# A small product ahead of each run of 448-column products, in an attention and mixing kernel on one core

## The chip, the cores and the metric

The kernel runs on one core of a Trainium2 chip (trn2). The metric is the device time of one execution in microseconds, lower is better; the time of a kernel is the median of several runs. One run of each kernel is also recorded by the hardware profiler, and everything that is said of single instructions below comes from such a record.

## The reference

Two stages in float32. Causal attention over 4 batches of 12 heads, 448 positions of width 64; then a mixing stage on the result x of 448 by 768 for each batch:

```python
scores = where(mask, -1e9, scale * q @ k.T); attn = softmax(scores); x = attn @ v
theta = x @ w_theta                       # 448x768 times 768x768
zr, zi = x * cos(theta), x * sin(theta)
y = w_tok_r @ zr + w_tok_i @ zi           # over the 448 positions
u = x + y
out = u + maximum(u @ w_ch, 0)            # 448x768 times 768x768
```

## The kernel before

All data lie with a channel or a position on the 128 partitions. Float32 accuracy is kept by splitting each operand into a high and a low part of a type that TensorE takes in one pass, and adding three products: high by high, high by low, low by high. So each block of a matrix product is three TensorE instructions with the same output, the first two with the same stationary operand (weights, `lhsT`). Each TensorE instruction of the program (a matmul) becomes two in the record: a load of its 128 weight columns (LDWEIGHTS, on the row of the engine that the profile calls PEld) and the product itself (MATMUL, on PE), also where the weights are those of the instruction before.

The parts that TensorE runs:

- attention: scores (lines 614 and 627, tiles `s`, `t`, `m`), transposes of the softmax weights by a product with the identity (line 672, 128 columns), the sums' transposes (line 646), and the products with v (line 698, 64 weight columns);
- `theta` (line 750): 384 columns a product, six blocks of 128 channels;
- `prep(g)` (lines 809 and 810): four transposes of x for channel block g, 128 columns each;
- `mix(g)` (line 829), for six channel blocks g of each of four batches: seven blocks of positions, three products each, all of 448 columns into one PSUM bank `y` of 512 columns, of which 448 are used and read;
- `pair` (line 927), twice, for two batches each: the last matrix product, done by a scheme that needs seven instead of eight half-size products, each named `product(w, ub, banks, ...)`: nine blocks of three products of 448 columns, into three PSUM banks `cp`, again 448 of 512 columns used. The very last product ends with 18 halves of 224 columns (line 937).

Vector, Scalar and GpSimd engines make the operands of these products and read the banks.

The order of all instructions is set by a planner in the kernel: `P.op` lists an operation with its estimated duration, its buffers and a due time, and `P.order()` simulates the engines and writes the program in the resulting order. A mix's seven operations are seven entries, so operations of the attention or of `theta` are put between them in the first batches; near the end little is left to put between, and the 448-column products follow each other without a break. What an entry emits (the inner function `mm`) is not seen by the planner, only its estimate `3 * pe(S)`.

```python
            for c in range(NTK):
                def mm(c=c):
                    for n, (l, w2) in enumerate(((zh, 0), (zh, 1), (zl, 0))):
                        nc.tensor.matmul(out=y.t[:, 0:S], lhsT=l.t[:, c], rhs=wtk[:, c, w2], ...)
                tick(3 * pe(S))
                P.op("PE", 3 * pe(S), mm, [(zh, i), (zl, i), (bwtk, (c, 0)), (bwtk, (c, 1))], [y])
```

Of the kernel before, what the change touches and what calls it, by code (L numbers as in the profile page):

```python
# [382 lines left out]
def attention_moe_kernel(  # L383
# [9 lines left out]
    nc = tc.nc  # L393
    B, NP, S = kq.shape[0], kq.shape[1], out.shape[2]
# [34 lines left out]
    def buf(ring, shape, dtype=F32, name=None):  # L429
        def make():  # L430
            if ring in ("s", "t", "xo", "m"):
                pool = psum
            elif ring in in_moe:
                pool = moe
            elif ring == "xT":
                pool = xpool
            elif ring == "rd":
                pool = dram
            elif ring in ("ub", "q1", "ot", "wf"):
                pool = o_pool[0]  # L440
            else:
                pool = apool
            return pool.tile(shape, dtype, tag=ring, name=name or ring, bufs=rings[ring])
        return P.buf(ring, make)
# [11 lines left out]
    wtk = wpool.tile([128, NTK, 2, S], F32R, name="wtk")  # L456
# [5 lines left out]
    def pe(n):  # L462
        return {128: 85, 256: 118, 384: 173.7, 448: 203.3, 512: 236}[n]

    def dv(n):
        return n / 0.96 + 68
# [13 lines left out]
    def dma(fns, nbytes, r=(), w=(), pr=None, after=(), row=1792, near=False, act=False):  # L480
        def run():
            for f in fns():
                (nc.scalar if act else nc.sync).dma_start(out=f[0], in_=f[1])
        n = nbytes[0]
        o = P.op("ACT" if act else "SP", 530 if n == 1 else 615.0 * n, run, r, w, lat=0, pr=pr, after=after)
        o.wire = nbytes[1] * (0.047 + 12 / row) / 16 * (1.2 if near else 1.0)
        return o
# [219 lines left out]
    th_last = []  # L707


    def batch(b, t0, rate):  # L710
        x = xT[b]
        R = [buf("R", [128, 4, HW]) for _ in range(2)]
# [4 lines left out]
        def tick(c):  # L717
            clock[0] += c * (KN["MR3"] if b < B - 1 and clock[0] > tau(NH) else rate)
            P.now = clock[0]
# [103 lines left out]
        def mix(g):  # L823
            zh, zl = zs[g]
            y = buf("m", [128, 512], F32, "y")
            for c in range(NTK):
                def mm(c=c):
                    for n, (l, w2) in enumerate(((zh, 0), (zh, 1), (zl, 0))):
                        nc.tensor.matmul(out=y.t[:, 0:S], lhsT=l.t[:, c], rhs=wtk[:, c, w2],  # L829
                                         start=(c == 0 and n == 0), stop=(c == NTK - 1 and n == 2))  # L830
                i = 0 if c < 4 else 1
                tick(3 * pe(S))
                P.op("PE", 3 * pe(S), mm, [(zh, i), (zl, i), (bwtk, (c, 0)), (bwtk, (c, 1))], [y])
            xk = [(x, (g, 0)), (x, (g, 1))]
            P.op("DVE", dv(S), lambda: nc.vector.tensor_tensor(
                out=x.t[:, g], in0=y.t[:, 0:S], in1=x.t[:, g], op=ALU.add), [y], xk)
            if b < B - KN["XT"]:
                dma(lambda: [(spill[b].t[:, g], x.t[:, g])], (1, 229376), xk, [(spill[b], g)])
# [32 lines left out]
    def pair(ba, bb, xa, xb, t0, rate, wb, ws, after, banks, rq, ro, end=False):  # L871
# [44 lines left out]
        def product(w, ub, banks, first, inner=True, half=None):  # L916
            wt, wk = w
            for x in range(NC):
                for y in range(NC):
                    m, c = (y, x) if inner else (x, y)  # L920

                    if m == NC - 1 and not inner:
                        break

                    def mm(m=m, c=c):
                        for n, (w2, a) in enumerate(((0, 0), (0, 1), (1, 0))):
                            nc.tensor.matmul(out=banks[m].t[:, 0:S], lhsT=wt()[:, c, w2, 128 * m:128 * m + 128],  # L927
                                             rhs=ub[c].t[:, a], start=(first and c == 0 and n == 0),
                                             stop=(c == NC - 1 and n == 2), skip_group_check=True)
                    clock[0] += 3 * pe(S) * rate  # L930
                    P.now = clock[0]
                    P.op("PE", 3 * pe(S), mm, [(ub[c], 0), (ub[c], 1)] + wk(c), [banks[m]])
            for z in range(0 if inner else 2):
                for c in range(NC):
                    def mm(c=c, z=z):
                        for n, (w2, a) in enumerate(((0, 0), (0, 1), (1, 0))):
                            nc.tensor.matmul(out=(half if z else banks[NC - 1]).t[:, 0:H2], lhsT=wt()[:, c, w2, 128 * NC - 128:128 * NC],
                                             rhs=ub[c].t[:, a, H2 * z:H2 * z + H2], start=(z == 1 and c == 0 and n == 0),
                                             stop=(c == NC - 1 and n == 2), skip_group_check=True)
                    clock[0] += 330 * rate  # L940
                    P.now = clock[0]
                    P.op("PE", 330, mm, [(ub[c], 0), (ub[c], 1)] + wk(c), [half if z else (banks[NC - 1], 0)])
# [58 lines left out]
        if end:  # L1001
            half = buf("s", [128, 512], F32, "cp")
            P.op("DVE", dv(H2), lambda: nc.vector.tensor_tensor(
                out=u2.t[:, NC - 1, H2:S], in0=Z[NC - 1].t[:, H2:S], in1=u2.t[:, NC - 1, H2:S], op=ALU.add),
# [34 lines left out]
    for b in range(B):  # L1039
        for p in range(NP):  # L1040
            load_pair(NP * b + p)
            attend(NP * b + p)
        if b == B - 1:
            att_ops = [o for o in P.ops[n_att:] if any(u.ring in ATT or u.ring[0] in "ep" for u in o.bufs)]
            P.now = tau(NH)

            def switch():
                att.close()
                o_pool.append(ctx.enter_context(tc.tile_pool(name="o", bufs=1)))
                for n in range(4):  # L1050
                    o_pool.append(o_pool[0].tile([128, NC, 2, HW], F32R, name=f"wa{n}", tag=f"wa{n}"))
            sw = P.op("X", 0, switch, after=att_ops)
            bw = [fixed(None) for _ in range(4)]
            for n in range(4):
                fetch(n, n % 2, 0, n // 2, lambda n=n: o_pool[1 + n], bw[n], TA + KN["E0"] + KN["ER"] * n, [sw])
            ws_t = wth.rearrange("p a b n -> p (a b n)")
            step = NC * 2 * HW
            wv = [ws_t[:, step * i:step * i + step].rearrange("p (c w n) -> p c w n", c=NC, w=2) for i in range(4)]
            bs = [fixed(t) for t in wv]
            wb = [((lambda n=n: o_pool[1 + n]), (lambda c, n=n: [(bw[n], (c, 0)), (bw[n], (c, 1))])) for n in range(4)]  # L1060
            ws = [((lambda i=i: wv[i]), (lambda c, i=i: [(bs[i], (c, 0)), (bs[i], (c, 1))])) for i in range(4)]
            first = pair(1, 2, xT[1], xT[2], TA + KN["O0"], KN["OR"], wb, ws, [sw],
                         (("s", "s", "t"), ("t", "xo", "s"), ("s", "t", "t"), ("xo", "s", "s")), "q1", "ot")
            next(first)
        t0 = tau(KN["HL"] + H * b + 2) + KN["M0"]
        end = batch(b, t0, KN["MR"] if b < B - 1 else KN["MR2"])
        if b < NC:
            channel(b, end + KN["C0"])
# [79 lines left out]
```

## Time and profile before

| | |
|---|---|
| time, median of 3 runs | 455.54 us (455.35 to 457.2) |
| time of the profiled execution | 456.17 us |
| its span, first to last instruction | 454.4 us |
| outside of the span | 1.8 us |
| TensorE products (PE) | 444.1 us busy, 2651 instructions |
| TensorE weight loads (PEld) | 367.0 us busy, 2651 instructions |
| VectorE, ScalarE, GpSimd | 362.5, 254.4, 50.5 us busy |
| granted TensorE clock, mean | 0.996 |

Busy time is the union of an engine's instructions. A product's recorded duration holds its way through the array as well, so that consecutive products overlap in the record: the time that one costs is the step from its start to the next one's start, and a merged row of n products gives it as its length over n. The chain of waits counts that step.

### The profile page before, as it was taken

What the parts mean: (1) busy time and instruction counts of PE and PEld (TensorE: products, weight loads), DVE (VectorE), ACT (ScalarE), POOL (GpSimd) and SP (SyncE); (2) the same over time, 40 slices, a digit from 0 to 9 for tenths busy, and PEclk for the clock granted to TensorE, in tenths of its full rate; (3) what the DMA queues carried; (4) which work ended last, traced back from release to release, by engine and by line L of the source; (5) the groups of instructions that cost most, each with busy time, mean ns of one, the idle gap of its engine ahead of it and who ended that gap; (6) DMA issues with size and microseconds to landing.
All of it is one profiled execution on the core that took longest, in us unless ns stands there. A gap on an engine that the chain in (4) does not pass through costs nothing.

```text
span 454.4 us, 7734 instructions
## 1 busy us (share of the span) xinstructions
PE 444.1 (98%) x2651; PEld 367.0 (81%) x2651; DVE 362.5 (80%) x953; ACT 254.4 (56%) x634; POOL 50.5 (11%) x51
## 2 busy tenths in 40 slices
PE   7979999999999999999999999999999999999996
PEld 3646667887777897887877998799999999999996
DVE  3999999669899856598979447896676999879976
ACT  5988797579965545289657217872125725322320
POOL 1022322000000010000002000021000023332320
PEclk9998999999999999999999999999999999999999
DMA  8886665213355363032350400132422331126114
GB/s 285 321 275 223 189 217 159 95 48 109 111 184 200 111 228 100 6 101 93 100 183 27 160 0 12 42 115 79 179 70 71 87 120 53 38 93 212 61 40 143
DMA packets 32391, 56.10 MB, mean 123 GB/s; under 512 B 11576, under 2 KB 23136, under 8 KB 32352
## 3 DMA queue, kind: packets, MB, share of 16 engines
q1 hardware_dynamic: 32064, 55.35, 37.5%
q8 instruction: 21, 0.34, 0.3%
q10 hardware_dynamic: 288, 0.26, 0.2%
q14 instruction: 18, 0.15, 0.1%
HBM read 42.34 MB, written 11.69 MB: 119 GB/s over the span
## 4 chain that ended last, share of the span: by engine, by line
PE 91%; DMA 4%; DVE 3%; issue 1%; SPq 0%; ACT 0%; DVEq 0%; ACTq 0%
PE y L829 23%; PE th L750 20%; PE cp L927 17%; PE xo L698 9%; PE t L672 8%; PE s L627 4%; PE s L614 3%; PE t L627 2%; PE xp L809 2%; DMA raw<-w_theta 2%; DMA kk<-kq 1%; DMA raw<-w_tok 1%; DVE e L633 1%; PE xo L646 1%; PE m L627 1%; PE xp L810 1%
## 5 line engine op out<-in xcount | busy, mean ns | idle before, releaser
L750 PE MATMUL th<-wth,xs 128*128 128x384 f32 x528 | 105.9, 345 | 0.0
L829 PE MATMUL y<-wtk,zh 128*128 128x448 f32 x336 | 101.0, 381 | 0.0
L750 PEld LDWEIGHTS th<-wth,xs 128*128 128x128 f32 x528 | 90.3, 188 | 5.0 <-issue 1.8
L636 ACT ACTIVATE e<-e,sm 128x384 f32<-128x384 f32 (+2 forms) x144 | 72.0, 501 | 28.0 <-DVE sm L633 27.4
L829 PEld LDWEIGHTS y<-wtk,zh 128*128 128x128 f32 x336 | 59.5, 188 | 6.4 <-issue 1.8
L829 PE MATMUL y<-wtk,zl 128*128 128x448 f32 x168 | 61.5, 366 | 0.0
L698 PE MATMUL xo<-pt,vs 128*64 128x448 f32 (+3 forms) x384 | 47.7, 387 | 0.3 <-ACT rs L648 0.3
L672 PE MATMUL t<-ident,e 128*128 128x128 f32 x288 | 44.7, 277 | 0.8 <-ACT pt L500 0.8
L698 PEld LDWEIGHTS xo<-pt,vs 128*64 128x64 f32 x384 | 25.1, 136 | 24.4 <-issue 14.3
L500 ACT COPY pt<-t 128x384 f32<-128x384 f32 (+2 forms) x73 | 34.5, 489 | 18.2 <-PE t L672 16.0
L927 PE MATMUL cp<-ub,wth 128*128 128x448 f32 x207 | 44.1, 367 | 0.0
L633 DVE CUSTOM_DVE_ANT_0 e<-s,mask 128x128 f32<-128x128 f32 (+2 forms) x94 | 37.0, 415 | 8.7 <-PE s L627 7.7
L672 PEld LDWEIGHTS t<-ident,e 128*128 128x128 f32 x288 | 34.4, 141 | 10.6 <-issue 2.9
L927 PEld LDWEIGHTS cp<-ub,wth 128*128 128x128 f32 x207 | 38.8, 188 | 3.7 <-issue 0.2
L927 PE MATMUL cp<-ub,wa 128*128 128x448 f32 x162 | 35.5, 367 | 0.0
L829 PEld LDWEIGHTS y<-wtk,zl 128*128 128x128 f32 x168 | 31.5, 188 | 2.8
L927 PEld LDWEIGHTS cp<-ub,wa 128*128 128x128 f32 x162 | 30.2, 188 | 2.6
L502 DVE COPY pt<-t 128x512 f32<-128x512 f32 (+2 forms) x47 | 27.5, 593 | 2.6 <-PE t L672 1.7
L636 ACT ACTIVATION_READ_ACCUMULATOR e<-e,sm 128x1 f32 x144 | 27.0, 188 | 0.0
L627 PE MATMUL s<-kk 64*128 64x384 f32 (+2 forms) x188 | 26.7, 399 | 0.0
L508 POOL TENSOR_TENSOR zc<-zc 128x384 f32<-128x384 f32 x6 | 6.0, 1009 | 178.6 <-DVE zc L530 178.0
L627 PEld LDWEIGHTS s<-kk 64*128 64x128 f32 x188 | 17.9, 190 | 9.1 <-issue 1.6
(115 smaller groups left out, 683.9 us busy)
## 6 DMA issues: line engine op xcount, KB each, us to landing
kk<-kq SPq DMA_DIRECT2D x23, 480.0 KB, 6.8
vs<-v SPq DMA_DIRECT2D x24, 256.0 KB, 3.7
raw<-w_theta SPq DMA_DIRECT2D x6, 768.0 KB
raw<-w_ch SPq DMA_DIRECT2D x6, 768.0 KB
wd<-zc SPq DMA_DIRECT2D x6, 768.0 KB
wf<-wd SPq DMA_DIRECT2D x24, 192.0 KB, 2.6
raw<-w_tok SPq DMA_DIRECT2D x7, 448.0 KB
rb<-rd SPq DMA_DIRECT2D x24, 112.0 KB, 2.8
```

The lines of the kernel that those rows point to most:

```text
L500: alts.append((e, ac(n, 0 if psum else 1), lambda: nc.scalar.copy(out=o(), in_=i())))
L502: alts.append((e, dv(n) if psum else dv2(n), lambda: nc.vector.tensor_copy(out=o(), in_=i())))
L614: nc.tensor.matmul(out=s.t[:, 0:S], lhsT=kp.t[:, S + MQ:S + KW], rhs=kp.t[:, 0:S])
L627: nc.tensor.matmul(out=s.t[:, c0:c0 + w], lhsT=kp.t[own, S + 128 * i:S + 128 * i + 128], rhs=kp.t[own, 0:w])
L633: P.op("DVE", dv(w) + 8, lambda m0=m0, c0=c0, w=w, s=s, e=e, c=c: nc.vector.tensor_tensor_reduce(out=e.t, in0=s.t[:, c0:c0 + w], in1=mask[ ...
L636: P.op("ACT", ac(w, 2.5), lambda e=e, c=c: nc.scalar.activation(out=e.t, in_=e.t, func=AF.Exp, scale=-1.0, bias=sm.t[:, 0, c:c + 1], accum ...
L672: nc.tensor.transpose(ps.t[:, 128 * n:128 * n + 128], e.t[:, c:c + 128], ident)
L698: nc.tensor.matmul(out=xo.t[64 * a:64 * a + 64, 128 * j:S], lhsT=vs.t[:, c:c + D], rhs=pt.t[:, a, slot(j):slot(j) + w], start=(j == 0), st ...
L750: nc.tensor.matmul(out=th.t[:, 0:HW], lhsT=l, rhs=wth[:, p, w2, c0:c0 + HW], start=(p == 0 and n == 0), stop=(p == KD - 1 and n == len(ops ...
L809: nc.tensor.transpose(xp.t[:, t], x.t[:, g, 128 * t:128 * t + 128], ident)
L829: nc.tensor.matmul(out=y.t[:, 0:S], lhsT=l.t[:, c], rhs=wtk[:, c, w2], start=(c == 0 and n == 0), stop=(c == NTK - 1 and n == 2))
L927: nc.tensor.matmul(out=banks[m].t[:, 0:S], lhsT=wt()[:, c, w2, 128 * m:128 * m + 128], rhs=ub[c].t[:, a], start=(first and c == 0 and n == 0),
```

## The change

Ahead of the first of the 21 products of each `mix`, and ahead of the first of the 27 products of each `product` of a `pair`, one more product is issued (`nudge`). It has the same weights as the product behind it, the first 16 or 64 columns of the same moving operand, and writes columns 448 to 463 or 448 to 511 of the same bank, which nobody reads. In `mix` it has 64 columns for odd g and 16 for even g; in `product` it has 16. The default arguments `x=x, y=y` in `product` bind the two loop counters, so that only the first of the nine blocks has it. That is 24 in the mixes (12 of each size) and 14 in the pairs, 38 in all, and 38 weight loads with them. The planner's estimates and due times are the same, and the order of all other instructions on every engine is as before.

```diff
+    def nudge(o, l, r, n, first=True):
+        nc.tensor.matmul(out=o[:, S:S + n], lhsT=l, rhs=r[:, 0:n], start=first, stop=False, skip_group_check=True)
+
...
             for c in range(NTK):
                 def mm(c=c):
+                    if c == 0:
+                        nudge(y.t, zh.t[:, 0], wtk[:, 0, 0], 64 if g % 2 else 16)
                     for n, (l, w2) in enumerate(((zh, 0), (zh, 1), (zl, 0))):
...
-                    def mm(m=m, c=c):
+                    def mm(m=m, c=c, x=x, y=y):
+                        if x == y == 0:
+                            nudge(banks[m].t, wt()[:, c, 0, 128 * m:128 * m + 128], ub[c].t[:, 0], 16, first)
                         for n, (w2, a) in enumerate(((0, 0), (0, 1), (1, 0))):
```

TensorE's program at the start of the first batch's first mix (g = 0), which stands behind the four transposes of `prep`. Before:

```order
L809 MATMUL xp<-ident,xT 128x128 x3
L810 MATMUL xp<-ident,xd 128x128
L829 MATMUL y<-wtk,zh 128x448 x2
L829 MATMUL y<-wtk,zl 128x448
L672 MATMUL t<-ident,e_1185 128x128
```

And with the change (line 711 is `nudge`, and line 834 is what line 829 was):

```order
L812 MATMUL xp<-ident,xT 128x128 x3
L813 MATMUL xp<-ident,xd 128x128
L711 MATMUL y<-wtk,zh 128x16
L834 MATMUL y<-wtk,zh 128x448 x2
L834 MATMUL y<-wtk,zl 128x448
L672 MATMUL t<-ident,e_1185 128x128
```

One product of 16 columns stands between the last transpose and the mix; nothing else moved. Near the end, where the last mixes run among the products of the first pair (in the span of before this is at 378 to 391 us), TensorE's program before:

```order
L829 MATMUL y<-wtk,zl 128x448
L927 MATMUL cp<-ub,wth 128x448 x9
L829 MATMUL y<-wtk,zh 128x448 x2
L829 MATMUL y<-wtk,zl 128x448
L927 MATMUL cp<-ub,wth 128x448 x45
L829 MATMUL y<-wtk,zh 128x448 x2
L829 MATMUL y<-wtk,zl 128x448
```

And with the change:

```order
L834 MATMUL y<-wtk,zl 128x448
L711 MATMUL cp<-ub,wth 128x16
L934 MATMUL cp<-ub,wth 128x448 x9
L834 MATMUL y<-wtk,zh 128x448 x2
L834 MATMUL y<-wtk,zl 128x448
L934 MATMUL cp<-ub,wth 128x448 x21
L711 MATMUL cp<-ub,wth 128x16
L934 MATMUL cp<-ub,wth 128x448 x24
L711 MATMUL y<-wtk,zh 128x64
L834 MATMUL y<-wtk,zh 128x448 x2
L834 MATMUL y<-wtk,zl 128x448
```

Here the small products stand in the middle of an unbroken row of 448-column products: two at the start of a `product`, one at the start of a mix.

## Rows read from the trace of the kernel before

**Rows 1.** The page: span, busy time, granted clock by slice, chain of waits by engine.

```profile
span 454.4 us, 7734 instructions
...
PE 444.1 (98%) x2651; PEld 367.0 (81%) x2651; DVE 362.5 (80%) x953; ACT 254.4 (56%) x634; POOL 50.5 (11%) x51
...
PEclk9998999999999999999999999999999999999999
...
PE 91%; DMA 4%; DVE 3%; issue 1%; SPq 0%; ACT 0%; DVEq 0%; ACTq 0%
```

**Rows 2.** Busy time by stage: us, PE, PEld, DVE, ACT, POOL, PEclk, DMA share, GB/s.

```profile
108.00:160.00 52.00, 52.00 (x345) 40.23 (x345) 46.26 (x132) 36.66 (x100) 1.05 (x2) 1.00 0.43 144
160.00:250.00 90.00, 90.00 (x581) 74.16 (x581) 68.47 (x201) 56.46 (x149) 3.32 (x4) 1.00 0.33 104
...
380.00:450.00 70.00, 70.00 (x349) 64.13 (x348) 60.32 (x106) 17.43 (x33) 17.17 (x15) 1.00 0.28 94
```

**Rows 3.** The chain of waits at the end of the program: start us, us, what.

```profile
407.93 40.95 PE cp L927 x201
448.88 0.02 issue
448.90 0.64 DVE u L962
```

**Rows 4.** The chain of waits, seven unbroken stretches of 448-column products.

```profile
111.24 1.82 PE y L829 x9
...
296.95 6.09 PE y L829 x30
...
308.18 3.09 PE cp L927 x15
...
366.24 4.26 PE y L829 x21
...
375.69 2.47 PE y L829 x12
...
380.65 9.30 PE cp L927 x45
...
406.07 1.86 PE y L829 x9
```

**Rows 5.** The chain of waits, a long stretch of 384-column products.

```profile
182.67 8.32 PE th L750 x48
```

**Rows 6.** Timeline of weight loads at the end of one mix: start us, us, what.

```profile
154.04 0.30 PEld L829 LDWEIGHTS y<-wtk,zh 128*128 128x128 f32 x2
154.35 0.19 PEld L829 LDWEIGHTS y<-wtk,zl 128*128 128x128 f32 x1
```

**Rows 7.** The chain of waits over 128-column transposes in front of a mix.

```profile
152.28 0.55 PE t L672 x5
152.82 0.33 PE xp L809 x3
```

**Rows 8.** Timeline of the last 224-column products, loads and products.

```profile
448.50 2.18 PEld L937 LDWEIGHTS cp<-ub,wth 128*128 128x128 f32 x18
448.70 2.16 PE L937 MATMUL cp<-ub,wth 128*128 128x224 f32 x18
```

**Rows 9.** Timeline of a long stretch of 448-column products, loads and products.

```profile
380.28 9.28 PEld L927 LDWEIGHTS cp<-ub,wth 128*128 128x128 f32 x45
380.49 9.46 PE L927 MATMUL cp<-ub,wth 128*128 128x448 f32 x45
```

**Rows 10.** Timeline of two consecutive weight loads inside the 201 products.

```profile
412.32 0.19 PEld L927 LDWEIGHTS cp<-ub,wa 128*128 128x128 f32 x1
412.58 0.19 PEld L927 LDWEIGHTS cp<-ub,wa 128*128 128x128 f32 x1
```

**Rows 11.** Timeline of single products at the start of one mix in batch 1.

```profile
246.72 0.36 PE L829 MATMUL y<-wtk,zh 128*128 128x448 f32 x1
246.92 0.36 PE L829 MATMUL y<-wtk,zl 128*128 128x448 f32 x1
```

**Rows 12.** Timeline where products of 128 and of 64 weight columns meet.

```profile
157.65 0.37 PE L829 MATMUL y<-wtk,zl 128*128 128x448 f32 x1
157.95 0.60 PE L698 MATMUL xo<-pt,vs 128*64 128x448 f32 x2
```

## The prediction

> **What bounds the kernel now.** I read the page first [rows 1]: TensorE's products are busy for 444.1 of 454.4 us, the granted clock is at nine tenths or more in every slice but the fourth, and 91% of the chain of waits that ends last is TensorE's. A mean can hide stages with another limit, so next came the busy time by stage [rows 2]: from 108 us, where the first of the added products would stand, PE is busy for the whole of each stage (52.00 of 52.00, 90.00 of 90.00, 70.00 of 70.00), while VectorE has 11% to 24% to spare and ScalarE more. Third, the chain at the end [rows 3]: an unbroken piece of 201 products of line 927, 40.95 us long, then the last additions of VectorE. So from 108 us on a microsecond that TensorE takes longer is a microsecond of the end, and one that it saves is saved, as long as the other engines keep up.
>
> Then I asked what a 448-column product costs, in steps from start to start. The chain's unbroken pieces give two values [rows 4]: 9.30 us for 45 is 0.2067, 1.86 for 9 is 0.2067, but 4.26 for 21 is 0.2029 and 6.09 for 30 is 0.2030. The clock is the same, 1.00 [rows 2], and so are the instructions. So there are two gaits, a long one (0.2067) and a short one (0.2029), 2% apart. The 201 products at the end, with 0.2037 [rows 3], begin in the long one and go on in the short one: inside them two weight loads stand 0.26 us apart [rows 10] where 0.2066 is usual ((9.28 - 0.19) over 44 steps, [rows 9]), and from there on the gait is short. For 384 columns the step is 8.32 over 48, 0.1733 [rows 5]. A small product can act on nothing else that I see than this gait: it gives the run behind it another start.
>
> **What the change adds.** 38 products, 38 weight loads, no new work on another engine, no transfer; the order is otherwise as before. Three terms.
>
> *The price of one.* The record of before has no product of 16 or 64 columns with 128 weight columns, so it is bounded. What counts is whether its weight load or that of the next product is hidden. In a long stretch the loads have the products' own step, and the row of 45 loads begins 0.21 us ahead of its 45 products [rows 9], which is one step: the load for a product begins as the product before it begins, and never earlier, though it lasts 0.19 and nothing else uses the loader. So one set of weights can wait behind the one in use and no second. Behind a small product, then, the weights of the first real product begin to load only when the small product begins, and what is left bare is a load's length less the small product's own columns. That length shows where products are too short to cover it: the two first loads of a mix behind transposes begin 0.30 - 0.19 = 0.11 us apart [rows 6]; transposes with 128 columns step by 0.55 over 5 and 0.33 over 3, 0.110 both [rows 7]; at the end the 224-column products' loads step by 0.112, (2.18 - 0.19 - 0.20) over 16, the first step being one behind a 448-column product [rows 8]. That it is the load that sets these steps, and not the columns, is seen from the transposes: 64 columns more cost 0.2029 - 0.1733 = 0.030 us (0.033 in the long gait), so 128 columns account for at most 0.066 of their 0.110. I take 0.110 for each, for 16 and 64 columns alike (0.008 and 0.03 of columns lie inside it). The lower end is a price of columns alone, 26 x 0.008 + 12 x 0.031 = 0.6 us in all; the upper one is a load plus the 0.09 us that a change of the kind of product costs where 448-column products give way to those with 64 weight columns (0.30 instead of 0.21, [rows 12]), 38 x 0.20 = 7.6 us. The value that I take is that of the nearest rows, with the same weights and type: 38 x 0.110 = 4.18 us.
>
> The Trainium skill speaks against this price and so for the change: "TensorE: Matmul & The Clock Gate", section "Back-to-back issue gap", gives products of 1 to 64 columns about 60 cycles, a floor of some 25 ns from start to start. By it the 38 would cost 38 x 0.025 = 0.95 us, and the sum below would be 456.4. The same section says that such a figure leaves out the weight load, and the transposes' 0.110 us [rows 7] side with that caveat.
>
> *The gait of the runs behind them.* In the first two batches a nudge stands ahead of only 3 to 6 products before something else comes between, so 12 of them can move next to nothing. From 291 us on the stretches are long. Fourteen pieces of the chain there have the long gait, from 3.09 us for 15 to 1.86 for 9 [rows 4], 47.08 us for 228 products together. All in the short gait they would take 46.26, so 0.82 is to be had, and up to 0.17 of the last 201: 1.0 us at best. Six pieces are in the short gait, from 6.09 us for 30 to 4.26 for 21 [rows 4], 114 products in 23.13 us; were these and the last 201 to fall into the long one, that would cost 0.43 + 0.60, 1.0 us at worst. Which is likelier? A nudge gives its run a start that waits for weights. So does a start behind transposes [rows 6], and of the 21 stretches of six or more products that begin so (the first 1.82 us for 9, the last 2.47 for 12, [rows 4]) 10 fall into the short gait and 11 into the long one. For a nudge in the middle of long-gait products the late load [rows 10] speaks a little for the short gait, since there one bare interval was enough to leave the long one, and the 186 or so long-gait products between 378 and 412 us have seven nudges ahead of them. I take a gain of 0.1 us, with 1.0 to either side.
>
> *What hides it.* Nothing: the added products carry the waits that the first real product carried, so a nudge runs when that product could have run, and PE has no idle time from 108 us on [rows 2] to put it in. Behind each nudge everything on TensorE is 0.11 us later, and the other engines' work that follows from it shifts along.
>
> The sum: +4.18 - 0.1 = +4.1 us. Against the profiled execution (span 454.4, 1.8 outside, 456.17 in all) that is 458.5 of span and 460.2 of time; that execution was 0.63 us above the median of the three runs, so on the median 455.54 the forecast is **459.6 us**, 0.9% slower, and the range of this case 458.5 to 460.8 (the gait's 1.0 us either way, and a price of 0.108 to 0.113).
>
> **Rivals.** *The small product is nearly free.* If the second load, of the same weights, could run ahead behind the small one or be left out, only the columns would count: 0.6 us less 0.1, 456.0, and between 455.0 and 457.0 with the gait. For it: the weights are the same as those of the next product. Against it: each split block already has two products in a row with the same weights, and both are loaded, two loads 0.11 us apart [rows 6]. The rule of the skill named above comes out here too, at 456.4. Chance 0.12.
>
> *The runs get a still shorter gait, and it isn't slower.* Single steps below 0.2029 exist: at the start of a mix in batch 1 two products stand 246.92 - 246.72 = 0.20 us apart [rows 11]. The 543 products of the pieces named above now take 47.08 + 23.13 + 40.95 = 111.16 us, 0.2047 each. If a nudge made them all go at 0.200, 2.6 us would come back of the 4.18 and the time would be 457.1, inside the 0.5%; the price is paid in full at 0.197. Against it: the lowest mean of a stretch in [rows 4] is 0.2022; the shorter steps come singly. Chance 0.03.
>
> *The small product costs more than a load.* Its step and that behind it could each be as at a change of kind [rows 12], 0.20 us for each nudge, 7.6 in all: 463.0. Against it: from 448 to 224 columns, with the same weights' width, no such gap is seen [rows 8]. Chance 0.05.
>
> **How the numbers follow.** Forecast 0.80, nearly free 0.12, dearer 0.05, shorter gait 0.03. About 0.5%, 2.3 us, is what a measurement of this kernel tells from no change; the bounds are 453.3 and 457.8. The forecast's case lies above the upper one throughout, as does the dearer one: slower 0.85. The free case and most of the short gait lie within: same 0.13, faster 0.02. The range reaches from the forecast's 458.5 to 460.8 down to the top of the free case, 457.0, and up to 461.2; it leaves out the free case, the dearer one and some of the third.
>
> **What would show it.** In the profile of the changed kernel PE and PEld should have 38 instructions more each, and each nudge of line 711 followed by the next weight load's end: its own load and the next one begin 0.11 us apart behind transposes, and in the middle of a stretch the product behind a nudge begins 0.11 us after it. The last long stretch then begins later by about 3 us and has seven breaks of 0.11 us. The gait of each stretch is read from the chain, piece by piece; short everywhere would bring the time to 458.6, long everywhere to 460.8. VectorE's, ScalarE's and GpSimd's busy time should stay as it is. The prediction is wrong if the step behind a nudge is near 0.03 us (then the weights didn't have to wait), if stretches of 448 columns fall under 0.201 in the mean, or if new idle time of PE appears ahead of a nudge.

## The result, and the profile after

The changed kernel takes 459.33 us in the median of 7 runs (458.73 to 460.33), the kernel before 455.62 in its 7 (454.1 to 457.45): a ratio of 1.0067, with a 95% interval from 1.0045 to 1.009 (the two medians by themselves give 1.0081). It is slower by 0.7%. The forecast was 459.6, with a range from 457.0 to 461.2. In some executions of either kernel the granted clock falls from 2.4 to 1.2 GHz for a short spell in the first 50 us, and they take about 2 us longer (of the kernel before 4 beside 31 others, medians 457.86 and 455.82), so the ratios scatter more than the parts of the traces compared below.

The page of the changed kernel, the lines that answer to [rows 1]:

```profile
span 458.5 us, 7811 instructions
...
PE 447.5 (98%) x2689; PEld 371.3 (81%) x2689; DVE 363.3 (79%) x953; ACT 254.9 (56%) x634; POOL 50.5 (11%) x51
...
PE 89%; DMA 4%; DVE 4%; issue 1%; SPq 0%; ACT 0%; DVEq 0%; ACTq 0%
```

38 instructions more on PE and on PEld (2689 against 2651), and the other engines do what they did. The span is 4.1 us longer, but 0.8 of that lies ahead of the first small product, in the loading at the start. To see the changed part alone, the timeline of products where it begins in the kernel before:

```profile
108.88 0.27 PE L810 MATMUL xp<-ident,xd 128*128 128x128 f32 x1
108.91 0.65 PE L829 MATMUL y<-wtk,zh 128*128 128x448 f32 x2
```

and in the changed kernel, where it begins and where it ends:

```profile
109.64 0.27 PE L813 MATMUL xp<-ident,xd 128*128 128x128 f32 x1
109.66 0.26 PE L711 MATMUL y<-wtk,zh 128*128 128x16 f32 x1
109.78 0.65 PE L834 MATMUL y<-wtk,zh 128*128 128x448 f32 x2
...
452.84 2.16 PE L944 MATMUL cp<-ub,wth 128*128 128x224 f32 x18
```

From the last transpose ahead of the first mix to the 18 halves at the end ([rows 8] has them at 448.70) it was 448.70 - 108.88 = 339.82 us and is 452.84 - 109.64 = 343.20: 3.38 more. The medians differ by 3.7 and the ratio gives 3.1 (2.1 to 4.1), which agrees, and the 3.38 are what has to be explained.

**The price.** A small product in the middle of a stretch, timeline of loads and of products of the changed kernel:

```profile
387.89 0.19 PEld L711 LDWEIGHTS cp<-ub,wth 128*128 128x128 f32 x1
388.10 0.89 PEld L934 LDWEIGHTS cp<-ub,wth 128*128 128x128 f32 x5
```

```profile
388.10 0.17 PE L711 MATMUL cp<-ub,wth 128*128 128x16 f32 x1
388.12 1.05 PE L934 MATMUL cp<-ub,wth 128*128 128x448 f32 x4
```

The small product's load begins one step ahead of it, under the product before (387.89 for 388.10). The load for the next product begins at 388.10, as the small product itself does, and not earlier. The record gives the next product an early start (388.12), but it can't stream before its weights are there: its step is 0.285 us instead of 0.203 (recorded starts, as all steps below that no row shows). Small product and long step together, 0.027 + 0.285, are 0.109 us more than one short step; read so, all 17 places behind a 448- or 384-column product cost 0.10 to 0.12. Behind transposes the 19 places show 0.111 to 0.112 from the small product to the next, and at the two places behind scores the next load begins 0.108 after the small product's. 38 x 0.1095 is 4.16 us.

**The gait.** The chain of waits of the changed kernel, stretches with their small product:

```profile
299.08 6.27 PE y L834 x30
...
305.80 4.36 PE y L834 x21
...
402.70 3.72 PE cp L934 x18
...
415.07 4.96 PE cp L934 x24
...
432.40 6.30 PE cp L934 x30
...
446.82 6.20 PE cp L934 x30
```

Less the 0.1 that the piece holds of the small product, 6.20 for 30 is 6.10, the short gait, and 6.30 is 6.20, the long one. The mix at 299.08 went from short (6.09, [rows 4]) to long (6.27); the 24 at 415.07 are short. Summed over all steps between 448-column products, what they take beyond 0.2027 us each fell from 1.31 us to 0.81: 0.50 back. With 0.19 from steps at the start of `theta` stretches, which shift too, 4.16 - 0.50 - 0.19 is 3.47; measured were 3.38.

**A wait that hides one of them.** Ahead of the last product of the second `pair` the loads of the kernel before pause:

```profile
441.51 0.80 PEld L927 LDWEIGHTS cp<-ub,wth 128*128 128x128 f32 x4
442.51 5.97 PEld L927 LDWEIGHTS cp<-ub,wth 128*128 128x128 f32 x30 [0.21 <-issue]
```

The load at 442.51 begins 0.40 us after the one ahead of it instead of 0.20, and the two steps there take 0.508 us instead of 0.405. In the changed kernel the small product stands at this place (its stretch is the one at 446.82 above). Its load is late as well, but under a running product, and the same stretch of the program takes 0.514. So of this one's price 0.10 was there before, and 3.47 - 0.10 is the 3.38 measured, to 0.01.

### The profile page after: what moved, and what is told of

It is laid out like the page before. It is cut to its first block, busy times and chain, and to the rows that moved or that the text cites. A ratio compares the mean times of both kernels' runs of the same rounds, so it can differ in the third digit from the quotient of the medians.

```text
span 458.5 us, 7811 instructions
## 1 busy us (share of the span) xinstructions
PE 447.5 (98%) x2689; PEld 371.3 (81%) x2689; DVE 363.3 (79%) x953; ACT 254.9 (56%) x634; POOL 50.5 (11%) x51
## 4 chain that ended last, share of the span: by engine, by line
PE 89%; DMA 4%; DVE 4%; issue 1%; SPq 0%; ACT 0%; DVEq 0%; ACTq 0%
PE y L834 23%; PE th L753 19%; PE cp L934 17%; PE xo L698 8%; PE t L672 8%; PE s L627 4%; PE s L614 3%; PE t L627 2%; PE xp L812 2%; DMA raw<-w_theta 2%; DMA kk<-kq 1%; DMA raw<-w_tok 1%; DVE e L633 1%; DVE zw L527 1%; PE xo L646 1%
```

## The experiments

Two numbers of each trace are compared besides the time. *Changed part*: from the last transpose ahead of the first mix to the start of the very last product, worked out from recorded starts. *Long-gait excess*: the sum over the steps between 448-column products of what each takes beyond 0.2027, without the first step of a stretch and the steps that hold a wait.

| | small products | changed part, us | excess, us | ratio to before (95%) |
|---|---|---|---|---|
| before, two traces | 0 | 341.71, 341.94 | 1.31, 1.39 | |
| the change, two traces | 38 | 345.09, 345.04 | 0.81, 0.86 | 1.0067 (1.0045 to 1.009) |
| in the pairs alone | 14 | 342.99 | 0.77 | 1.0029 (1.0016 to 1.0043) |
| two at each place | 76 | 348.57 | 0.17 | 1.0165 (1.0117 to 1.0213) |
| with 32 weight columns | 38 | 344.36 | 0.25 | 1.0054 (1.0038 to 1.0071) |
| mixes, 224 columns | 24 | 343.58 | 0.73 | 1.0066 (1.0042 to 1.0089) |
| all of 64 columns | 38 | 344.65 | 0.55 | 1.0038 (1.0021 to 1.0055) |
| pairs split 224 and 224 | 0 | 341.72 | 0.62 | 0.9985 (0.9964 to 1.0006) |
| pairs split 256 and 192 | 0 | 341.98 | 0.49 | 0.9971 (0.995 to 0.9993) |
| pairs and mixes split 224 | 0 | 341.81 | 0.26 | 0.9999 (0.9981 to 1.0018) |

**Half of them.** The small products of the mixes taken out again:

```diff
-                    if c == 0:
-                        nudge(y.t, zh.t[:, 0], wtk[:, 0, 0], 64 if g % 2 else 16)
```

> The 24 small products of the mixes are taken out, the 14 of the pairs stay. Theory (each small product costs the bare weight load of the product behind it, 0.110 us, wherever it stands): 14 x 0.110 = 1.5 us, so a time of 457.2, between 456.1 and 458.2 with the gaits of the stretches (1.0 us either way), and 0.11 us from each small product to the product behind it, less what its stretch's gait gives back. Rival (the price belongs to the places behind transposes, where the mixes start, and in the middle of a stretch the load is hidden): about 0.01 us each, 455.7. Both expect 14 more PE instructions than the kernel before.

457.01 us, ratio 1.0029. The changed part is 1.2 us longer than before; 14 x 0.109 less 0.58 of gait is 0.95, and 0.2 more is a longer wait in the attention, ahead of the first small product (it is shown with the splits below). The rival, which hid the price in the middle of a stretch, would have gained on the kernel before.

**Twice as many.**

```diff
-        nc.tensor.matmul(out=o[:, S:S + n], lhsT=l, rhs=r[:, 0:n], ...)
+        for _ in range(2):
+            nc.tensor.matmul(out=o[:, S:S + n], lhsT=l, rhs=r[:, 0:n], ...)
```

> Two equal small products at each of the 38 places, 76 in all. Theory: 76 x 0.110 = 8.4 us, 464.0 with 1.0 either way for the gaits; the second one costs as much as the first. Rival (the price is one for breaking a stretch, whatever stands in the break): the second costs its columns alone, 0.6 us for all 38, so about 460. Second rival (the same weights a third time can be held): also about 460.

462.07 us in the median, ratio 1.0165 (one of the four runs took 466.69; the medians give 1.0135). The chain of waits (line 712 is the small product here):

```profile
428.15 0.12 PE cp L712 x2
428.27 5.57 PE cp L935 x27
433.84 0.12 PE cp L712 x2
433.96 6.18 PE cp L935 x30
440.14 0.12 PE cp L712 x2
440.26 4.96 PE cp L935 x24
```

The chain puts 0.12 us on the two and another 0.1 on the piece behind them (5.57 for 27 is 0.10 over 27 x 0.2027): the second costs as much as the first. Neither rival's 460 came about. The time is 0.9 us below the low end expected, because almost every stretch is in the short gait: the excess is 0.17, so 8.3 - 1.2 = 7.1 is to be expected of the changed part, and 6.7 was measured; 0.3 of what is missing came back at the starts of `theta` stretches.

**A shorter load for the small product.**

```diff
-        nc.tensor.matmul(out=o[:, S:S + n], lhsT=l, rhs=r[:, 0:n], ...)
+        nc.tensor.matmul(out=o[0:32, S:S + n], lhsT=l[:, 0:32], rhs=r[:, 0:n], ...)
```

> The small products use the first 32 of their 128 weight columns, so that their own load is a quarter as long, about 0.03 us; the loads of the products behind them stay as they are. Theory (the load that is bare is that of the product behind, which can begin only when the small product begins): where the small product stands behind a 448- or 384-column product, its own load is hidden and 0.11 us stays, 17 places; behind transposes and scores, 21 places, the load of the first product was bare before already, and only the small product's own 0.03 us comes on top. 17 x 0.11 + 21 x 0.03 = 2.5 us, 458.1 with 1.0 either way. Rival (the price is the small product's own load): 38 x 0.03 = 1.1 us, 456.7, and 0.03 in the middle of a stretch. Second rival (a fixed price for a product, whatever is loaded): 4.2 us as in the change, and 0.11 at both kinds of place. The steps of the two kinds of place tell the three apart better than the time.

458.24 us, ratio 1.0054. The time alone would side with the theory, but for the wrong reason; the loads show it. Behind transposes, in the middle of a stretch, and behind scores:

```profile
108.38 0.14 PEld L813 LDWEIGHTS xp<-ident,xd 128*128 128x128 f32 x1
108.48 0.11 PEld L711 LDWEIGHTS y<-wtk,zh 128*32 128x32 f32 x1
108.59 0.30 PEld L834 LDWEIGHTS y<-wtk,zh 128*128 128x128 f32 x2
...
386.20 0.11 PEld L711 LDWEIGHTS cp<-ub,wth 128*32 128x32 f32 x1
386.40 0.70 PEld L934 LDWEIGHTS cp<-ub,wth 128*128 128x128 f32 x4
...
161.20 0.11 PEld L711 LDWEIGHTS y<-wtk,zh 128*32 128x32 f32 x1
161.23 0.30 PEld L834 LDWEIGHTS y<-wtk,zh 128*128 128x128 f32 x2
```

In the middle of a stretch nothing changed: 0.109 us, though the small product's own load is a quarter as long. So the price isn't its own load, and that rival falls. Behind transposes I had expected 0.03, and it is 0.109 at all 19 places: the next load begins 0.11 us after the small one's (108.48, 108.59), just as with a full load in the changed kernel:

```profile
109.64 0.19 PEld L711 LDWEIGHTS y<-wtk,zh 128*128 128x128 f32 x1
109.75 0.30 PEld L834 LDWEIGHTS y<-wtk,zh 128*128 128x128 f32 x2
```

The short load should be done long before, but the last transpose is not; it takes 0.11 us by itself, and the small product has to wait for it as it does for a 448-column product. The record of the kernel before bears this out. There a float32 product of 448 columns (scores, line 614) takes two records, in the chain:

```profile
117.86 0.75 PE s L614 x2
```

That is 0.375 us for one record of 448 columns, 0.84 ns a column, and 128 columns at that rate are 0.107. Where nothing runs ahead, at the two places behind scores, the next load begins 0.03 us after the short one (161.20, 161.23), and there the price is 0.03. That speaks against a fixed price for an instruction, which 0.109 at all other places would fit as well: what is bare is a load, and its length goes with its columns. No run made the load of the product behind shorter, so that it is this load's length which sets the price elsewhere rests on where the loads begin. In the changed kernel the two loads at the same place behind scores are 0.11 apart:

```profile
162.52 0.19 PEld L711 LDWEIGHTS y<-wtk,zh 128*128 128x128 f32 x1
162.63 0.30 PEld L834 LDWEIGHTS y<-wtk,zh 128*128 128x128 f32 x2
```

**More columns.** Only in the mixes, 224 columns, which the first real product then overwrites; those of the pairs are out:

```diff
-                        nudge(y.t, zh.t[:, 0], wtk[:, 0, 0], 64 if g % 2 else 16)
+                        nudge(y.t, zh.t[:, 0], wtk[:, 0, 0], 224, True, 0)   # 0: first column of the output
```

> Only the 24 small products of the mixes, and each has 224 columns, written to columns 0 to 223 of the bank, which the first real product then overwrites. Theory (columns lie inside the load of the next product as long as they are shorter than it): 0.112 us each, as the steps of the 224-column products at the end of the kernel before, 2.7 us, 458.3 with up to 0.6 either way for the gaits. Rival (a price of about 0.10 for the instruction, and its columns on top at 0.46 ns each): 0.20 each, 4.8 us, 460.4.

459.06 us in the median of five (457.56 to 460.24), ratio 1.0066, 0.2 us above the range expected. The changed part is 1.8 us longer than before, 0.3 below it; 24 x 0.109 less 0.62 of gait is 2.0, and 0.19 came back at the starts of `theta` stretches. Its first place in the timeline of loads reads like the one with 16 columns, 0.11 us to the next load:

```profile
111.07 0.19 PEld L711 LDWEIGHTS y<-wtk,zh 128*128 128x128 f32 x1
111.18 0.30 PEld L834 LDWEIGHTS y<-wtk,zh 128*128 128x128 f32 x2
```

From the recorded starts, behind transposes the small product and the step behind it add up to 0.395 to 0.401 us against 0.396 to 0.403 in the change. Fourteen times the columns cost nothing more. Columns on top of a fixed price (0.20 each) are out.

**One size.** All of 64 columns:

```diff
-                            nudge(banks[m].t, ..., ub[c].t[:, 0], 16, first)
+                            nudge(banks[m].t, ..., ub[c].t[:, 0], 64, first)
```

and 64 for every g.

> All 38 small products have 64 columns. Theory (columns inside the bare load cost nothing, and the gait behind a small product is set by the moment at which the next load begins, not by its columns): 0.110 us each as in the change, a time within 0.7 us of the change's, and in the pairs the same kind of stretch goes the same way as with 16: long gait before it gives short gait behind it. Rival (the gait is set by the number of columns): stretches behind 64 columns in the pairs fall otherwise than behind 16, most of them to the other gait.

458.22 us, ratio 1.0038, and 1.1 us below the change's time where 0.7 was expected at most. The price is the same, the gaits aren't, and neither theory got them right. The chain, the stretches that were long in the change (3.72 for 18 and 6.30 for 30):

```profile
402.11 3.64 PE cp L934 x18
...
431.74 6.16 PE cp L934 x30
```

Both are short now (6.16 less 0.08 is 6.08). In the middle of a stretch all 17 places lead to the short gait with 64 columns; in the change three of the 17, all with 16 columns, lead to the long one, the same three in both traces. Where the stretch ahead was long, the stretch behind was short with either size. So the columns do matter to the gait, a little, and the size chosen in the pairs was the worse one. The recorded starts show where: the short gait repeats every five steps, and a small product of 16 columns that comes right behind the steps 0.199, 0.207, 0.202, 0.203, 0.202 led to the long gait at all eight such places (two traces of the change and that of the pairs alone), while at the 19 others behind a short stretch it led to the short one. With 64 columns the three places behind these same steps led to the short one.

**The traces again.** Both kernels unchanged, for a second trace of each.

> The kernel before, unchanged, for a second trace: is the gait of a stretch the same in every execution? Theory (the gait is set by the moment of the start, which depends on waits and transfers before it): some stretches of six or more products have the other gait than in the first trace, and the long-gait excess differs by several tenths of a microsecond from its 1.3 us. Rival (the gait belongs to the place in the program): the same stretches are long, the excess is 1.3 us.

> The changed kernel, unchanged, for a second trace. Theory: 0.11 us behind each small product again. Behind a small product of 16 columns in the middle of a stretch the gait is short wherever the stretch before was long; where it was short it can go either way, by the step of the short gait at which it comes. The long-gait excess is 0.8 us in the first trace and differs here by some tenths.

One execution each, 454.19 and 459.9 us. The chain of the kernel before, second trace:

```profile
294.85 6.09 PE y L829 x30
...
378.56 9.30 PE cp L927 x45
...
405.84 41.05 PE cp L927 x201
```

These stretches have the same gait as in [rows 3, 4], to 0.1 us, and the excess is 1.39 against 1.31; that of the change is 0.86 against 0.81, where some tenths were expected. For nearly all of the program my theory (that waits and transfers shift the gait from one execution to the next) falls: of the stretches of six or more products, 36 before and 50 in the change, three of six to nine products, all ahead of 125 us, have the other gait in the second trace, and else the gait belongs to the place in the program. The 0.1 us are the exception, where the theory fits. They come from the last 30 products behind the pause shown above, whose loads in the second trace are:

```profile
440.41 6.08 PEld L927 LDWEIGHTS cp<-ub,wth 128*128 128x128 f32 x30 [0.20 <-issue]
```

The pause is 0.01 us shorter, and less the first step of 0.108 the loads step by 0.2065 us, where they had 0.2026 in the first trace (5.97 in place of 6.08). So behind a wait the gait can differ between two executions of one program.

**The same start for less.** If a break can shorten the gait, it should not cost a load. No small product; the first 448-column product of each of the pairs is made in two parts:

```diff
                         for n, (w2, a) in enumerate(((0, 0), (0, 1), (1, 0))):
+                            for q in parts(x == y == n == 0):    # [0:224], [224:448]; else [0:448]
-                            nc.tensor.matmul(out=banks[m].t[:, 0:S], ..., rhs=ub[c].t[:, a], ...)
+                                nc.tensor.matmul(out=banks[m].t[:, q], ..., rhs=ub[c].t[:, a, q], ...)
```

> No small products. Instead the first 448-column product of each of the 14 products of the pairs is made as two of 224 columns, with the same weights and the same sums. Theory: two steps of 0.112 us stand in the place of one of 0.203, so the price is 0.02 us each, 0.3 us in all, instead of 0.110 each, and the stretch gets another start as behind a small product. If long-gait stretches turn short as they do behind the small products, up to 0.8 us come back: the time lies between 0.6 us under the kernel before and 1.0 over it, 455.5 as the middle. Rival (a break costs a full load wherever it is put): 1.5 us more than before, less the gait.

> As the split into 224 and 224 columns, with 256 and 192. The load behind the 256 columns is covered, the one behind the 192 is about 0.01 us longer than they are: 0.02 to 0.03 us for each split, 0.4 us in all, and another start of the stretch. If the gait is set by the moment of the start, the stretches fall otherwise than with 224; the time is within 1.0 us of the kernel before.

> As the split into 224 and 224, in the 24 mixes too: 38 splits. Theory: 38 x 0.02 = 0.8 us for the splits, and up to 1.0 us back from the gaits: between 0.2 us under the kernel before and 1.8 over it. Rival (a full load for each): 4.2 us more than before, as in the change.

455.49, 454.93 and 456.15 us beside 455.99 for the kernel before; ratios 0.9985, 0.9971 and 0.9999 (256 and 192 was expected within 1.0 us of the kernel before, and is 1.06 under it). The price is as small as expected: in the middle of a stretch a split into 224 and 224 columns costs 0.02 us and one into 256 and 192 costs 0.025 to 0.04 (recorded starts), and the rival with a full load is out. The gait turned too. The chain with 256 and 192 columns, at the places of [rows 4] with 9.30 for 45:

```profile
379.83 9.14 PE cp L931 x46
...
406.73 41.05 PE cp L931 x208
```

9.14 us for 45 products of which one is split. With 256 and 192 every stretch of six or more products right behind a split is short. The 201 products at the end, seven of them split, take 41.05: they were short for the greater part before, so the splits give nothing there. On the clock the 256 split has the best time, 0.3% under the kernel before with an interval that ends just short of one, but it is the best of three. Its whole changed part doesn't bear this out: 341.98 us is no shorter than the 341.71 and 341.94 of before. Two things cancel in it. From the last attention product (line 698, at 296 us) to the end, where the splits of the pairs stand, it takes 154.16 us and the two other split kernels 154.05 and 154.10, against 154.45 and 154.56 before: 0.3 to 0.5 won. Up to there, where 256 and 192 has no split, it takes 187.8 against 187.3 and 187.4. Of this loss 0.2 to 0.35 is one wait of the attention, ahead of the sums' transposes (line 646, at 228 us). In the waits of the weight loads, before and with 256 and 192:

```profile
PEld xo L646 <- issue: 0.2, 1, 0.2
PEld xo L646 <- PE y L832: 0.5, 1, 0.5
```

The step there takes 0.55 us in all three split kernels, 0.20 and 0.36 in the two traces of before, and 0.51 with small products in the pairs alone, where nothing is changed up to that place either. So the splits gain where they stand; what sets that wait was not found, and whether a split kernel is faster as a whole, by up to 0.3%, stays open.

## Why the prediction was right, and where it wasn't

*What bounds the kernel.* Right: TensorE has no idle time from 108 us on in the changed kernel either, no new wait came, and 3.38 us more on TensorE are 3.1 to 3.7 more at the end (by the ratio and by the medians). That nothing hides the price held at 37 of the 38 places; at the last one a wait of 0.10 us was there already.

*The price.* The sum had 38 x 0.110 = 4.18 us; measured 38 x 0.1095 = 4.16. The mechanism, one set of weights waits behind the one in use and no second, is what the loads show: at the 17 places behind 448- and 384-column products the load behind a small product begins 0.002 to 0.004 us after the small product does, and never ahead of it. The experiments exclude the rivals: not its own load (32 weight columns), not its columns (224), not a price of the break as such (two each), and, by the two places behind scores alone, not a fixed price of an instruction (0.03 there). One sign was badly chosen: the prediction was to be wrong "if the step behind a nudge is near 0.03 us", and in the middle of a stretch the recorded step is 0.027. The weights did have to wait all the same; it is the step after it, 0.285 us, that holds the wait. And one piece of the evidence was misread. "That it is the load that sets these steps, and not the columns, is seen from the transposes": the transposes' 0.110 [rows 7] is their own time, for a small product with a quarter of the load still waits 0.11 us behind one. I had scaled their columns by the steps of other products [rows 5], and transposes of plain float32 don't go at that rate. The two first loads of a mix [rows 6], the second of which begins when the transpose is done, are no evidence for the load's length either. That the number stood is luck in this part: a load of 128 columns happens to be as long, which the places behind scores show (162.52 and 162.63 above).

The Trainium skill, "TensorE: Matmul & The Clock Gate", section "LDWEIGHTS (loading the stationary operand)", gives a load the number of its columns over 1.2 in ns: 107 for 128 columns and 27 for 32. The traces agree, 0.11 and 0.03 us from one load to the next where nothing else holds it. The floor of 25 ns in the Trainium skill, same page, section "Back-to-back issue gap", by which the estimate was 456.4, is not what a small product costs here (0.109 us); the caveat of that section, that the weight load is left out, is the price. The transposes, which the prediction let "side with that caveat", say nothing on it.

*The gait.* A gain of 0.1 with 1.0 either way was forecast, and 0.5 came back (0.69 with the `theta` steps). That is the term that was mis-sized, within its bounds. The guess behind it, that long-gait stretches tend to turn short behind a small product because a bare load starts them anew, held at every place where a stretch was long ahead of it. What the prediction had to leave to chance, since the starts behind transposes were half and half, has turned out to be fixed by the place nearly everywhere; that the time came within 0.3 us of the forecast, while TensorE took 0.7 less than the sum (3.38 for 4.08), is in part the scatter of the times.

*The rivals.* Nearly free small products (456.0): out, by the loads. A still shorter gait (457.1): no stretch of twelve or more has a mean under 0.2018; single steps of 0.195 come at the start of a stretch. Dearer than a load (463.0): out, 0.109.

## What to carry to other kernels

In a busy row of products on TensorE, one more product that is shorter than its successor's weight load costs that load, about 0.11 us for 128 weight columns, whether it has 16 or 224 columns and even with the same weights: count loads, not columns. An effect worth 2% of a step (4 ns) needs more than 27 steps behind it to pay for such a product, and where a break is wanted, splitting a product in two parts of about a load's length costs 0.02 to 0.04 us instead. When two causes would give the same number, as the transposes' own time and the load did here, change one of them alone before building on either.

## What the runs showed of the hardware that was not expected

- Products of 448 columns in an unbroken stretch at the full granted clock go in one of two gaits, 0.2067 us for every step, or five steps of 0.203, 0.199, 0.207, 0.202 and 0.203 in turn, 0.2027 in the mean; a stretch keeps its gait for up to some 180 products. Which one it gets is with few exceptions the same in two executions at the same place and changes with what is issued ahead: two small products, or one with 32 weight columns, or a split into 256 and 192, led nearly always to the short one, one of 16 columns mostly, by the step of the five behind which it came. A load that came 0.05 us late turned a long gait short at no cost [rows 10], and behind a wait of 0.1 us the gait differed between two executions. Why was not found; 48 products of 384 columns in a row step by 0.1733 [rows 5].
- A transpose of 128 columns in float32 takes 0.109 us of TensorE by itself, with 128 or 32 weight columns loaded under it, more than half of a 448-column product.
- Weights are loaded again for each product also when they are those already in place (336 loads for the 336 products `y<-wtk,zh` of line 829, of which every second has the weights of the one ahead), and at most one set ahead.
